# Holding a weight transfer until values have landed, with a third score buffer and earlier gathers, in a fused block-sparse attention and MLP kernel

## The chip, the cores and the metric

One core of a Trainium2 chip runs the kernel. Times are device microseconds of one execution. A kernel is compared by the mean of its fast runs over the mean of the fast runs of the kernel before in the same rounds on the same chip, with a 95% interval. A ratio is therefore not quite the ratio of the medians that stand beside it.

Engines in the profile, by what they do in this kernel: PE multiplies matrices (PEld loads its weights), DVE does elementwise work, ACT exponentials and Gelu, POOL gathers, and SP and POOL issue DMA transfers. SPq and POOLq are the two DMA queues of those two issuers. The argument below takes it that each engine works through its own instructions in program order; where no run below tests this, it is the author's assumption.

## The reference

```python
def _attn_ref(q, k, v, sampled_blocks):          # (4, 8, 768, 64) each; blocks of 32, 24 of them
    scores = np.matmul(q, k.transpose(0, 1, 3, 2)) / np.sqrt(D)
    # kept: neighbouring blocks, first and last block row and column, 3 sampled blocks per block row
    scores = np.where(mask, scores, -1e9)
    attn = softmax(scores)                         # written out in the original
    return np.matmul(attn, v)

def _moe_ref(x, w_in, w_out):                      # x: (3072, 512); w_in: 512 x 2048; w_out: 2048 x 512
    h = x @ w_in
    return gelu_exact(h) @ w_out
```

## The kernel before

A batch of 768 rows is worked in two halves of 384. Each half has attention, then a hidden layer (w_in, Gelu), then an output layer (w_out) whose matmuls are woven between the attention steps of the next half. The first half of batch 0 computes **dense** scores with a mask folded in ("dense half"). Every other half gathers key and value blocks with POOL (tiles kg and v_gat). Values are first cast into `v_flat`, then three rotated copies of them are made by DMA, and the value gathers read those.

The parts that the argument touches:

```python
def load_v(b, eng, after=None):                   # one buffer for the values of a batch
    t = stv_pool.tile([P, NT, H, D], F32, tag="st_v", name="st_v")
    if after is not None:
        after.memset(t[:, :, 0:1, 0:1], 0.0)
    for n in range(NT):                           # rows of 64 f32 = 256 bytes
        eng.dma_start(out=t[:, n], in_=v[b, :, n * P:n * P + P].rearrange("h p d -> p h d"))
    return t
# ...
new_x(0, 0, st)
first_pair(0)                                     # transpose q and k of head pair 0
for c in range(2):
    load_w_in(c)                                  # POOL queue, at about 12 us
gather_iotas()
for hp in range(NPAIR):                           # dense half; first_pt has two buffers (hp % 2)
    for t in range(NT):
        first_scores(hp, t)                       # PE scores, ACT exp
        if t == 1 and hp > 0:
            first_weighted(hp - 1)                # PE: needs the cast values
        elif t == 3 and hp + 1 < NPAIR:
            first_pair(hp + 1)
            if hp == 0:
                for n in range(NT):
                    own_v(0, first_v, n, n + 1, dve)     # casts of batch 0's values
            elif hp == 1: ...                     # index arithmetic on DVE
            elif hp == 2: ...                     # rotation on SP, value indices on DVE
# ...
for c in range(2):
    load_w_out(c)
# ... first second half of attention, main list:
#     S0 D0 S1 E0 W0 D1 S2 E1 W1 D2 S3 E2 W2 D3 E3 W3
#     S scores, D dense scores, E dense weighting (tile od), W gathered weighting (tile og)
after[0] = own_steps(b + 1)                       # right behind S0: two casts of the next batch's
                                                  # values, then their rotation
```

Two buffers serve the results of E and W. E1 can therefore start only when DVE has normalised E0.

The softmax here doesn't subtract the row's maximum and nothing guards it: scores larger than these inputs give would overflow.

Of the kernel before, what the change touches and what calls it, by code (L numbers as in the profile page):

```python
# [11 lines left out]
BF16 = mybir.dt.bfloat16  # L12
# [3 lines left out]
AF = mybir.ActivationFunctionType  # L16
# [3 lines left out]
P = 128  # L20
# [3 lines left out]
NT = S // P  # L24
# [55 lines left out]
def kernel(  # L80
# [34 lines left out]
    def load_qk(b, which, n):  # L115

        t = st_pool.tile([P, NPAIR, NT * D], BF16, tag="st", name="st")
        src = {"q": q, "k": k}[which]
        pool.dma_start(
            out=t, in_=src[b, 4 * n:4 * n + 4].rearrange("h (p j) d -> p h (j d)", j=NT))  # L120
        return t
# [31 lines left out]
    def iota(out, pattern, base, mult):  # L153
        pool.iota(out, pattern=pattern, base=base, channel_multiplier=mult,
                  allow_small_or_imprecise_dtypes=True)
# [5 lines left out]
    def load_w_in(c):  # L161
        f = slice(1024 * c, 1024 * c + 1024)
        pool.dma_start(out=w_in_sb[:, :, f], in_=w_in_v[:, :, f])

    def load_w_out(c):
        pool.dma_start(out=w_out_sb[:, 8 * c:8 * c + 8, :], in_=w_out_v[:, 8 * c:8 * c + 8, :])
# [9 lines left out]
    pool.affine_select(out=ident, in_=ident, compare_op=ALU.not_equal, fill=1.0, base=0,  # L176
                       pattern=[[-1, P]], channel_multiplier=1)
    iota(blocks, [[1, NB]], 0, 0)
    for w, x in (("k", k), ("q", q)):
        pool.dma_start(out=st["st", w, 0][:, 2:4, :],  # L180
                       in_=x[0, 2:4].rearrange("h (p j) d -> p h (j d)", j=NT))
    for w in "kq":
        st["st", w, 1] = load_qk(0, w, 1)



    key_i = small("key_i", [1], I32)
# [50 lines left out]
    mask_x = small("mask_x", [NT, P], BF16, const)  # L238
    n_even = -(-(NULL + 1) * H * GW // DW)

    def gather_iotas():
        iota(mask_ka, [[4, 4], [1, NR]], 0, 0)
        iota(rowm, [[4, 4]], 3, 0)
        iota(cols, [[4, 3]], 3, 0)
        iota(qbt, [[1, NQ], [0, NR]], 1, 0)
        pool.memset(base_v, float(NULL))
        iota(base_v[96:128, 3::4], [[1, 5]], 0, 0)
        iota(base_v[96:128, 2:19:4], [[1, 5]], 7, 0)

    def gather_constants():  # L250

# [116 lines left out]
    def own_v(b, st_v, lo, hi, eng):  # L368
        n = slice(lo, hi)
        cast(eng, v_own[b % 2][:, n, :, 0:D], st_v[:, n])  # L370

    def rotate_v(b, r, eng):

        for lo, hi, src in ((0, P - 32 * r, 32 * r), (P - 32 * r, P, 0)):
            eng.dma_start(out=v_all[lo:hi, NT * r:NT * r + NT],
                         in_=v_own[b % 2][src:src + hi - lo])
# [117 lines left out]
    def dense_weighted(b, hp, st):  # L494

        od = og_pool.tile([P, 1, 2, VW], F32, tag="og", name="od")
        for t in range(NT):
# [3 lines left out]
        normalise(st["xd"][:, hp:hp + 1].rearrange("p m (h d) -> p m h d", h=2), od, 1)  # L501


    first_pt = [first.tile([P, NT, 2, HALF], BF16, name="first_pt"),
                v_gat[0].rearrange("p n h e -> p (n h e)")[:, 0:NT * 2 * HALF]
                .rearrange("p (t h c) -> p t h c", t=NT, h=2)]

    def first_scores(hp, t):
        s1 = sc_pool.tile([P, 2, 512], F32, tag="sc", name="s1")
        c = slice(t * P, t * P + P)  # L510
        for l, r_, first_ in ((onehot.rearrange("p n c -> p (n c)"),
                               barred.rearrange("p n c -> p (n c)"), True),
                              (st["k", hp], st["q", hp], False)):
            for h in range(2):
                r = slice(64 * h, 64 * h + 64)
                pe.matmul(s1[:, h, 0:HALF], lhsT=l[r, c], rhs=r_[r, 0:HALF],
                          start=first_, stop=not first_)
        act.activation(first_pt[hp % 2][:, t], s1[:, :, 0:HALF], AF.Exp, scale=scale)

    def first_weighted(hp):  # L520
        og = og_pool.tile([P, MH, 2, VW], F32, tag="og", name="og")
        for m in range(MH):
            for h in range(2):
                for t in range(NT):
                    pe.matmul(og[:, m, h, :], lhsT=first_pt[hp % 2][:, t, h, m * P:m * P + P],
                              rhs=v_own[0][:, t, 2 * hp + h, 0:VW],
                              start=(m == h == t == 0), stop=True, skip_group_check=True)
        normalise(st["x", 0][:, :, hp * P:hp * P + P].rearrange("p m (h d) -> p m h d", h=2),
                  og, MH)

    def new_x(b, hb, st):
        st["x", hb] = x_pool.tile([P, MH, D_MODEL], BF16, tag="x", name="x")
        st["xT", hb] = x_pool.tile([P, KIN, HALF], BF16, tag="xT", name="xT")
        if hb == (b == 0):
            st["xd"] = x_pool.tile([P, NPAIR, P], BF16, tag="xd", name="xd")
# [90 lines left out]
    def first_pair(hp):  # L626
        i = 2 * (hp % 2)
        for w in "kq":
            pair = st["st", w, hp // 2][:, i:i + 2, :]
            if hp == 0:  # L630
                act.copy(pair, first_st[w])
            transpose_qk(0, hp, w, pair, dve, st)
        for w in "kq":
            globals_qk(0, hp, w, pool, st)

    new_x(0, 0, st)
    first_pair(0)
    for c in range(2):
        load_w_in(c)
    gather_iotas()  # L640
    for hp in range(NPAIR):
        for t in range(NT):
            first_scores(hp, t)
            if t == 1 and hp > 0:
                first_weighted(hp - 1)
            elif t == 3 and hp + 1 < NPAIR:
                first_pair(hp + 1)
                if hp == 0:
                    for n in range(NT):
                        own_v(0, first_v, n, n + 1, dve)  # L650
                elif hp == 1:
                    gather_constants()
                    key_indices()
                    value_columns()
                elif hp == 2:
                    for r in range(1, 4):
                        dve.memset(v_all[:, NT * r:NT * r + 1, 0:1, 0:1], 0.0)
                        rotate_v(0, r, sp)
                    value_indices(0, dve)
                    value_indices(1, dve)  # L660
    first_weighted(NPAIR - 1)
    for m in range(MH):
        transpose_x(0, 0, m, st)
    clear_mask()
    for i in range(2):
        clear_globals(i, dve)
    for c in range(2):
        load_w_out(c)
    for i in range(2):
        mark_valid(i)  # L670
    first_ctx.close()
    g_pool = ctx.enter_context(tc.tile_pool(name="g_pool", bufs=1))
    os_pool = ctx.enter_context(tc.tile_pool(name="os_pool", bufs=3))

    sts[1]["st", "v"] = load_v(1, sp, dve)

    def load_batch(b):
        st = sts[b]
        for n in range(2):
            for w in "kq":  # L680
                st["st", w, n] = load_qk(b, w, n)

    def transpose_step(b, hp):
        i = 2 * (hp % 2)
# [11 lines left out]
    def global_steps(b):  # L696
        return [lambda: [global_v(b, s, dve) for s in range(4)]]
# [4 lines left out]
    for half in range(2 * B):  # L702
        b, hb = divmod(half, 2)
        nb_, nhb = divmod(half + 1, 2)
        more = b + 1 < B

        aux = []
        if half == 0:
            for t in kgl[1]:
                dve.memset(t, 0.0)  # L710
            aux = global_steps(0) + k_steps(0, 1, (0,)) + v_steps(0, 1)
            aux += k_steps(0, 1, range(1, NPAIR))
        elif hb == 0 and more:
            for hp in (0, 1):
                aux += t_steps(b + 1, (hp,)) + k_steps(b + 1, 0, (hp,))
        elif hb == 1 and more:
            if b == 0:
                aux = v_steps(1, 0)
            aux += global_steps(b + 1)
            for hp in range(2 * (b > 0), NPAIR):  # L720
                aux += t_steps(b + 1, (hp,)) + k_steps(b + 1, 0, (hp,))
            if b + 2 < B:
                sts[b + 2]["st", "v"] = load_v(b + 2, sp)
        for n, step in enumerate(spread(hidden_steps(b, hb, sts[b]), aux)):
            step()
        if half == 0:
            load_batch(1)

        fill = output_steps(b, hb, sts[b])
        if half + 1 == 2 * B:  # L730
            weave([], fill)
            break
        main = attention_steps(nb_, nhb, sts[nb_])
        after = {}
        if nhb == 1 and more:
            after[0] = own_steps(b + 1)
            if b > 0:
                after[3] = k_steps(b + 1, 1, (0,))
                after[4] = k_steps(b + 1, 1, (1,))
                after[len(main) - 4] = v_steps(b + 1, 0)  # L740
        elif nhb == 0:
            if nb_ + 1 < B:
                load_batch(nb_ + 1)
            after[0] = v_steps(nb_, 1) + k_steps(nb_, 1, range(2 * (b > 0), NPAIR))
        steps = []
        for n, (step, m) in enumerate(main):
            steps.append((step, m))
            steps += [(f, 0) for f in after.get(n, [])]
        weave(steps, fill)
# [30 lines left out]
```

## Time and profile before

| | before |
|---|---|
| median of 4 runs | 336.98 us (336.42 to 337.69) |
| span of the profiled run | 335.9 us |
| PE busy | 274.0 us, 82% |
| hidden layer 0 starts | 59.16 us |
| E1 starts | 89.17 us |

Stretches of the kernel before, cut at the start of E1. The columns are the stretch, its length, busy time and instructions of each engine, the mean granted PE clock, the DMA engines' mean busy share and GB/s.

```profile
core 0: us, PE busy (x) PEld busy (x) DVE busy (x) ACT busy (x) POOL busy (x), PEclk, DMA share, GB/s
0.00:89.17 89.17, 48.42 (x572) 29.48 (x573) 38.78 (x155) 35.02 (x45) 23.64 (x47) 0.85 0.78 152
89.17:335.90 246.73, 225.63 (x2991) 135.57 (x2988) 101.14 (x209) 120.95 (x161) 78.92 (x103) 1.00 0.38 82
```

PE works 48 of the first 89 us, but 226 of the last 247. About two thirds of PE's idle time (40.8 of 61.9 us) lie ahead of E1.

PE's waits of the kernel before, from 10 to 130 us (what waited, for whom, us in total, times, longest):

```profile
PE og L54 <- DVE v_flat L54: 12.4, 4, 10.0
PE s L54 <- POOL kg L54: 6.8, 1, 6.8
PE s L54 <- DVE v_flat L54: 4.9, 1, 4.9
```

The timeline places these waits (start, duration, engine, instruction, count, idle before it and what ended it). SPq and POOLq lines are transfers being issued.

```profile
2.22 17.09 SPq L54 DMA_DIRECT2D st_v<-in_v_dram  x6
12.38 1.49 POOL L54 DMA_DIRECT2D w_in_sb<-in_moe_w_in_dram  x2
29.41 0.43 DVE L54 CAST v_flat<-st_v 128x512 bf16<-128x512 f32 x1 [9.80 <-DMA st_v<-in_v_dram]
59.16 2.76 PE L54 MATMUL hp<-xT,w_in_sb 128*128 128x384 bf16 x16 [0.52 <-DVE xT L54]
69.70 1.66 POOL L54 INDIRECT_COPY v_gat<-v_flat,idx_v 128x1024 f32 x1 [9.03 <-issue]
80.37 1.10 DVE L54 CAST v_flat<-st_v 128x1536 bf16<-128x1536 f32 x1 [1.60 <-DMA st_v<-in_v_dram]
82.58 0.47 PE L54 MATMUL s<-tq,kg 64*128 64x32 bf16 x22 [6.83 <-POOL kg L54]
89.17 0.51 PE L54 MATMUL od<-v_flat,pd 128*128 128x130 bf16 x6
```

Batch 0's values, issued from 2.22 us, are only 1.6 MB, yet the fourth of their six casts waits until 29.41 and the last starts at 31.37. w_in was issued in between, at 12.38. Later kg makes PE wait until 82.58, because POOL did the value gathers (from 69.70) first. The last line is E1, which had to wait for nothing by itself.

### The profile page before, as it was taken

What the parts mean: (1) busy time and instruction counts of PE and PEld (TensorE: products, weight loads), DVE (VectorE), ACT (ScalarE), POOL (GpSimd) and SP (SyncE); (2) the same over time, 40 slices, a digit from 0 to 9 for tenths busy, and PEclk for the clock granted to TensorE, in tenths of its full rate; (3) what the DMA queues carried; (4) which work ended last, traced back from release to release, by engine and by line L of the source; (5) the groups of instructions that cost most, each with busy time, mean ns of one, the idle gap of its engine ahead of it and who ended that gap; (6) DMA issues with size and microseconds to landing.
All of it is one profiled execution on the core that took longest, in us unless ns stands there. A gap on an engine that the chain in (4) does not pass through costs nothing. (4 is left out here: it accounts for less than half of the span.)

```text
span 335.9 us, 8110 instructions
## 1 busy us (share of the span) xinstructions
PE 274.0 (82%) x3560; PEld 165.1 (49%) x3560; DVE 139.9 (42%) x364; ACT 156.0 (46%) x206; POOL 102.6 (31%) x149
## 2 busy tenths in 40 slices
PE   1712937881989979898999798999997999999995
PEld 0302514441655656464656464555564655555542
DVE  5221795502455727532553177326442453044001
ACT  2430633580542376246625663356346652663420
POOL 4410121134623446444415455232035341000000
PEclk9985878998799999999999999999999999999999
DMA  7996009996999608600769095004910000000001
GB/s 141 208 207 126 3 29 195 232 179 130 246 188 193 106 2 134 119 33 0 176 196 204 3 156 97 31 2 97 257 38 0 35 33 31 2 31 35 31 33 62
DMA packets 42131, 33.79 MB, mean 101 GB/s; under 512 B 26096, under 2 KB 36464, under 8 KB 42096
## 3 DMA queue, kind: packets, MB, share of 16 engines
q1 hardware_dynamic: 31024, 23.18, 28.1%
q0 software_dynamic: 11072, 10.09, 19.4%
q8 instruction: 28, 0.46, 0.6%
q14 instruction: 7, 0.06, 0.1%
HBM read 27.34 MB, written 6.29 MB: 100 GB/s over the span
## 5 line engine op out<-in xcount | busy, mean ns | idle before, releaser
L54 PE MATMUL op<-w_out_sb,g 128*128 128x512 bf16 x384 | 94.8, 383 | 0.0
L54 ACT ACTIVATE g<-hp 128x768 bf16<-128x768 f32 x64 | 51.7, 810 | 84.4 <-PE hp L54 84.4
L54 PE MATMUL hp<-xT,w_in_sb 128*128 128x384 bf16 x512 | 86.8, 327 | 1.6 <-ACT g L54 1.0
L54 PEld LDWEIGHTS <-w_in_sb 128*128 128x128 bf16 x512 | 49.1, 98 | 35.4 <-issue 2.3
L54 ACT ACTIVATE pt<-s 128x1024 bf16<-128x1024 f32 (+2 forms) x84 | 51.6, 687 | 28.0 <-PE s L54 14.4
L54 DVE TENSOR_TENSOR pt<-pt,mask_x 128x768 bf16<-128x768 bf16 x28 | 21.3, 762 | 85.8 <-ACT pt L54 85.7
L54 POOL INDIRECT_COPY kg<-tk,idx_k 128x704 f32 x28 | 34.9, 1248 | 62.8 <-issue 58.6
L54 POOL INDIRECT_COPY v_gat<-v_flat,idx_v 128x1024 f32 (+1 forms) x21 | 33.5, 1594 | 61.6 <-issue 35.3
L54 PEld LDWEIGHTS <-g 128*128 128x128 bf16 x384 | 33.9, 98 | 31.7 <-issue 0.5
L54 DVE COPY tk<-ps 128x768 bf16<-128x768 bf16 x16 | 15.3, 956 | 32.0 <-PE ps L54 32.0
L54 PEld LDWEIGHTS <-tk 64*128 64x128 bf16 (+1 forms) x312 | 15.1, 98 | 26.9 <-issue 19.1
L54 DVE COPY os<-op 128x512 f32<-128x512 f32 x24 | 16.5, 689 | 25.6 <-PE op L54 25.5
L54 ACT ACT_TABLE_LOAD x16 | 20.5, 1283 | 10.9 <-PE hp L54 5.3
L54 PE MATMUL s<-tq,tk 64*128 64x128 bf16 (+1 forms) x216 | 19.6, 260 | 6.2 <-DVE v_flat L54 4.9
L54 PE MATMUL ps<-ident,st 128*64 128x128 bf16 x384 | 15.7, 237 | 9.2 <-ACT st L54 9.2
L54 PE MATMUL s<-tq,kg 64*128 64x32 bf16 x616 | 12.2, 174 | 12.6 <-POOL kg L54 6.8
L54 PEld LDWEIGHTS <-pt 128*32 128x32 bf16 (+1 forms) x868 | 19.9, 97 | 2.9 <-issue 0.6
L54 POOL COPY kgl<-tk 64x64 bf16<-64x64 bf16 x32 | 8.1, 254 | 40.7 <-DVE tk L54 40.0
L54 PEld LDWEIGHTS <-st 128*64 128x64 bf16 x384 | 12.7, 120 | 14.8 <-ACT st L54 9.4
L54 ACT ACTIVATE v_gat<-s 128x768 bf16<-128x768 f32 x12 | 9.0, 809 | 23.1 <-PE s L54 23.1
L54 DVE TENSOR_TENSOR x<-og,rc 128x384 bf16<-128x384 f32 x32 | 17.8, 558 | 1.1
L54 PEld LDWEIGHTS <-kg 64*128 64x128 bf16 x616 | 11.3, 93 | 14.1 <-issue 7.1
(109 smaller groups left out, 241.9 us busy)
## 6 DMA issues: line engine op xcount, KB each, us to landing
st_v<-in_v_dram SPq DMA_DIRECT2D x24, 256.0 KB, 5.9
out_dram<-os SPq DMA_DIRECT2D x24, 256.0 KB, 2.5
v_flat<-v_flat SPq DMA_DIRECT2D x8, 594.0 KB, 7.0
v_flat<-v_flat SPq DMA_DIRECT2D x8, 396.0 KB, 5.5
st<-in_k_dram POOLq DMA_DIRECT2D x7, 384.0 KB, 8.7
st<-in_q_dram POOLq DMA_DIRECT2D x7, 384.0 KB, 10.3
w_in_sb<-in_moe_w_in_dram POOLq DMA_DIRECT2D x2, 1024.0 KB, 13.4
w_out_sb<-in_moe_w_out_dram POOLq DMA_DIRECT2D x2, 1024.0 KB, 22.0
```

Source lines behind the costliest of these rows:

```text
L54: return self._tc.keep_in_program_order(f(*args, **kwargs))
```

## The change

Its intent: let batch 0's values land before w_in starts, by giving w_in's target a small DVE write behind the casts, so that the transfer must wait for it. Keep PE and ACT busy meanwhile by running the scores up to three head pairs ahead of the weighting, in a third buffer (memory of the second gather tile, not yet in use). Bring forward the key gathers, w_out and batch 1's q and k. The diff also moves POOL's index patterns ahead of batch 0's q and k loads, which start about 1 us later for it (2.58 for 1.50 us); this is left out below. The core of the diff:

```diff
-    first_pt = [first.tile(...), v_gat[0]...]
+    first_pt = [first.tile(...)] + [... for t in v_gat]            # cut: three buffers, hp % 3
 ...
+    def after_values():
+        for n in range(NT):
+            own_v(0, first_v, n, n + 1, dve)
+        for c in range(2):
+            dve.memset(w_in_sb[:, 0:1, 1024 * c:1024 * c + 1], 0.0)
+            load_w_in(c)
+    def rotate_first():
+        for r in range(1, 4):
+            dve.memset(v_all[:, NT * r:NT * r + 1, 0:1, 0:1], 0.0)
+            rotate_v(0, r, sp)
     new_x(0, 0, st)
     first_pair(0)
-    for c in range(2):
-        load_w_in(c)
-    gather_iotas()
+    extra = {(0, 3): lambda: first_pair(1),
+             (1, 1): lambda: first_pair(2),
+             (1, 3): lambda: first_pair(3),
+             (2, 1): after_values,
+             (2, 3): lambda: [first_weighted(0), gather_constants(), key_indices()],
+             (3, 1): lambda: [first_weighted(1), load_w_out(0), load_w_out(1)]
+             + [f() for f in k_steps(0, 1, range(NPAIR))],
+             (3, 3): lambda: [first_weighted(2), rotate_first(), value_columns()]}
 ...
     for i in range(2):
         mark_valid(i)
+    load_batch(1)                                  # batch 1's q and k
 ...
-            aux = global_steps(0) + k_steps(0, 1, (0,)) + v_steps(0, 1)
-            aux += k_steps(0, 1, range(1, NPAIR))
+            aux = v_steps(0, 1) + global_steps(0)
 ...
-        if half == 0:
-            load_batch(1)                          # was behind hidden layer 0
```

More of the change, by code (lines that the diff above doesn't have):

```diff
@@ L178 @@
     iota(blocks, [[1, NB]], 0, 0)
-    for w, x in (("k", k), ("q", q)):
-        pool.dma_start(out=st["st", w, 0][:, 2:4, :],
-                       in_=x[0, 2:4].rearrange("h (p j) d -> p h (j d)", j=NT))
-    for w in "kq":
-        st["st", w, 1] = load_qk(0, w, 1)
     key_i = small("key_i", [1], I32)
@@ L239 @@
     n_even = -(-(NULL + 1) * H * GW // DW)
-    def gather_iotas():
-        iota(mask_ka, [[4, 4], [1, NR]], 0, 0)
-        iota(rowm, [[4, 4]], 3, 0)
-        iota(cols, [[4, 3]], 3, 0)
-        iota(qbt, [[1, NQ], [0, NR]], 1, 0)
-        pool.memset(base_v, float(NULL))
-        iota(base_v[96:128, 3::4], [[1, 5]], 0, 0)
-        iota(base_v[96:128, 2:19:4], [[1, 5]], 7, 0)
+    iota(mask_ka, [[4, 4], [1, NR]], 0, 0)
+    iota(rowm, [[4, 4]], 3, 0)
+    iota(cols, [[4, 3]], 3, 0)
+    iota(qbt, [[1, NQ], [0, NR]], 1, 0)
+    pool.memset(base_v, float(NULL))
+    iota(base_v[96:128, 3::4], [[1, 5]], 0, 0)
+    iota(base_v[96:128, 2:19:4], [[1, 5]], 7, 0)
+    for w, x in (("k", k), ("q", q)):
+        pool.dma_start(out=st["st", w, 0][:, 2:4, :],
+                       in_=x[0, 2:4].rearrange("h (p j) d -> p h (j d)", j=NT))
+    for w in "kq":
+        st["st", w, 1] = load_qk(0, w, 1)
     def gather_constants():
@@ L501, in dense_weighted @@
         normalise(st["xd"][:, hp:hp + 1].rearrange("p m (h d) -> p m h d", h=2), od, 1)
-    first_pt = [first.tile([P, NT, 2, HALF], BF16, name="first_pt"),
-                v_gat[0].rearrange("p n h e -> p (n h e)")[:, 0:NT * 2 * HALF]
-                .rearrange("p (t h c) -> p t h c", t=NT, h=2)]
+    first_pt = [first.tile([P, NT, 2, HALF], BF16, name="first_pt")]
+    for t in v_gat:
+        first_pt.append(t.rearrange("p n h e -> p (n h e)")[:, 0:NT * 2 * HALF]
+                        .rearrange("p (t h c) -> p t h c", t=NT, h=2))
     def first_scores(hp, t):
@@ L517, in first_scores @@
                           start=first_, stop=not first_)
-        act.activation(first_pt[hp % 2][:, t], s1[:, :, 0:HALF], AF.Exp, scale=scale)
+        act.activation(first_pt[hp % 3][:, t], s1[:, :, 0:HALF], AF.Exp, scale=scale)
     def first_weighted(hp):
@@ L524, in first_weighted @@
                 for t in range(NT):
-                    pe.matmul(og[:, m, h, :], lhsT=first_pt[hp % 2][:, t, h, m * P:m * P + P],
+                    pe.matmul(og[:, m, h, :], lhsT=first_pt[hp % 3][:, t, h, m * P:m * P + P],
                               rhs=v_own[0][:, t, 2 * hp + h, 0:VW],
@@ L634, in first_pair @@
             globals_qk(0, hp, w, pool, st)
-    new_x(0, 0, st)
-    first_pair(0)
-    for c in range(2):
-        load_w_in(c)
-    gather_iotas()
-    for hp in range(NPAIR):
-        for t in range(NT):
-            first_scores(hp, t)
-            if t == 1 and hp > 0:
-                first_weighted(hp - 1)
-            elif t == 3 and hp + 1 < NPAIR:
-                first_pair(hp + 1)
-                if hp == 0:
-                    for n in range(NT):
-                        own_v(0, first_v, n, n + 1, dve)
-                elif hp == 1:
-                    gather_constants()
-                    key_indices()
-                    value_columns()
-                elif hp == 2:
-                    for r in range(1, 4):
-                        dve.memset(v_all[:, NT * r:NT * r + 1, 0:1, 0:1], 0.0)
-                        rotate_v(0, r, sp)
-                    value_indices(0, dve)
-                    value_indices(1, dve)
-    first_weighted(NPAIR - 1)
-    for m in range(MH):
-        transpose_x(0, 0, m, st)
-    clear_mask()
-    for i in range(2):
-        clear_globals(i, dve)
-    for c in range(2):
-        load_w_out(c)
-    for i in range(2):
-        mark_valid(i)
-    first_ctx.close()
-    g_pool = ctx.enter_context(tc.tile_pool(name="g_pool", bufs=1))
-    os_pool = ctx.enter_context(tc.tile_pool(name="os_pool", bufs=3))
-    sts[1]["st", "v"] = load_v(1, sp, dve)
     def load_batch(b):
@@ L681, in load_batch @@
                 st["st", w, n] = load_qk(b, w, n)
+    def after_values():
[8 more added lines that the diff above has]
+            rotate_v(0, r, sp)
+    new_x(0, 0, st)
+    first_pair(0)
+    extra = {(0, 3): lambda: first_pair(1),
[6 more added lines that the diff above has]
+             (3, 3): lambda: [first_weighted(2), rotate_first(), value_columns()]}
+    for hp in range(NPAIR):
+        for t in range(NT):
+            first_scores(hp, t)
+            extra.get((hp, t), lambda: None)()
+    first_weighted(NPAIR - 1)
+    for m in range(MH):
+        transpose_x(0, 0, m, st)
+    value_indices(0, dve)
+    value_indices(1, dve)
+    clear_mask()
+    for i in range(2):
+        clear_globals(i, dve)
+    for i in range(2):
+        mark_valid(i)
+    load_batch(1)
+    first_ctx.close()
+    g_pool = ctx.enter_context(tc.tile_pool(name="g_pool", bufs=1))
+    os_pool = ctx.enter_context(tc.tile_pool(name="os_pool", bufs=3))
+    sts[1]["st", "v"] = load_v(1, sp, dve)
     def transpose_step(b, hp):
```

## The prediction

> **What bounds the kernel now.** The span is 335.9 us; PE is busy 82% (page, part 1). The stretch table puts nearly all idle PE time before 83 us: about 44 of the first 83 us busy, later stretches near full. The timeline and the waits name the holes:
> - 19.9 to 31.9: PE waits for the casts of the first batch's values, DVE for their transfers (11.9 us in four waits). Six value transfers issued from 2.2 us land up to 18.9 us after issue; the last three only when w_in has landed (issued 12.4, landing after 10.9 and 16.0 us).
> - 43.5 to 48.4: PE waits 4.9 us behind DVE's index arithmetic.
> - 75.7 to 82.6: PE waits 6.8 us for kg, which stands on POOL behind three value gathers that started at 69.7, after the rotation (issued 48.4 to 54.8) had landed beside w_out.
>
> Hidden layer 0 starts at 59.2, the first gathered weighting of its second half at 83.9, the second dense weighting (E1) at 89.2. From there PE is full, so the change is worth what it takes off E1.
>
> **Why values starve.** [...] beside w_in (2048 B) the values (256 B) move 24 against 182 GB/s; beside st (768 B) 50 against 140; rotation (6336 B) against w_out (1024 B) 200 against 45.
>
> **What the change does.** w_in waits for the casts; all pairs are transposed early; scores run three pairs ahead of the weighting; key gathers go ahead of the value gathers; w_out follows w_in at once; batch 1's q and k load at about 50 us instead of 89. Added work is two tiny memsets (0.06 us each). PE, ACT and DVE work stays.
>
> Estimates from these durations: values land at about 20 us, casts end at 25 (6 x 0.43), w_in is issued at 25 to 26. 24 exponentials of 0.755 us and the PE work between them end the dense half at about 35; value columns (4.5 us, now ahead of the last normalise) put hidden layer 0 at 42 to 44 (59.2 before). Rotation is issued at 34 to 36 and lands at 48 to 52; value gathers end at 58 to 62 (77.8 before). The 6.8 us wait for kg goes.
>
> **What catches the gain.** The transfers become one busy stretch from 26 us: w_in 2.1 MB, rotation 2.4, w_out 2.1, batch 1's q/k 1.6, its values 1.6. At the observed 165 to 250 GB/s this is about 49 us, so batch 1's values, starved behind w_out and q/k, land at about 76 (80.4 before). Their casts stand in DVE's order ahead of the second mask and the normalise that frees E1's buffer. So E1 starts at about 79, 10 us earlier rather than 16; PE idles some 8 to 10 us before it and restarts at a reduced clock (as at 80 to 90 us before, mean 0.66), costing about 2 us. Net 8 to 9 us.
>
> **Predicted: 328.5 us, range 321 to 334; faster by over 2% 0.68, within 2% 0.28, slower 0.04.**
>
> **What would show it.** No wait for st_v over 3 us before 30 us; w_in issued near 25; hidden layer 0 near 43; kg waits gone; a new DVE wait for batch 1's st_v landing near 76, and PE waiting for DVE in the second half's attention until about 79; unchanged stretches after it.
>
> **What would make it wrong.** If batch 1's values land before about 70 the gain is 13 to 16 us; if q/k and w_out starve them past 82, it is under 5. A late w_in (second half after 49 us)[...] would also cost.

The rates under "Why values starve" are worked out from the packet records of the kernel before. The sum: 10 us at E1 less about 2 for the clock, net 8 to 9, hence 328.5.

## The result, and the profile after

| | before | after | predicted |
|---|---|---|---|
| median of 4 runs | 336.98 us | 327.64 us (325.92 to 328.57) | 328.5 (321 to 334) |
| ratio of fast runs | | 0.9716 (0.9666 to 0.9765) | |
| span of the profiled run | 335.9 | 324.2 | |
| hidden layer 0 starts | 59.16 | 39.69 | 42 to 44 |
| last value gather of batch 0 ends | 77.75 | 60.63 | 58 to 62 |
| E1 starts | 89.17 | 75.65 | 79 |

The profiled run after was the fastest of the four, and the profiled run before (337.77 us, not one of the four in the table) was slower than all of those. So the gain in span (11.7 us) is larger than the gain of the medians (9.3 us).

The two stretches after, cut at E1 again:

```profile
0.00:75.65 75.65, 46.59 (x573) 27.14 (x574) 39.99 (x155) 36.70 (x48) 25.20 (x51) 0.87 0.98 178
75.65:324.20 248.55, 227.31 (x2988) 136.52 (x2987) 104.30 (x212) 119.11 (x158) 74.92 (x98) 0.99 0.35 82
```

E1 comes 13.5 us earlier, and what follows E1 takes 1.8 us longer (248.55 against 246.73). The DMA share ahead of E1 rose from 0.78 to 0.98. A share can exceed 1 (it is 1.13 from 38 to 52 us), so this doesn't mean that there was no pause: from 20 to 24 us, while w_in is held, it is 0.02.

PE's waits after, from 10 to 130 us:

```profile
PE od L54 <- DVE xd L54: 8.3, 1, 8.3
PE psx L54 <- DVE x L54: 3.6, 1, 3.6
PE hp L54 <- ACT g L54: 3.3, 1, 3.3
```

The waits for values, for kg and for the index arithmetic are gone. Three others took their place. The largest is E1 (tile od) waiting for DVE's normalise of E0 (tile xd). The timeline after shows where that comes from:

```profile
21.10 2.17 DVE L54 CAST v_flat<-st_v 128x512 bf16<-128x512 f32 x6
23.60 1.48 POOL L54 DMA_DIRECT2D w_in_sb<-in_moe_w_in_dram  x2 [1.61 <-DVE w_in_sb L54]
39.69 5.28 PE L54 MATMUL hp<-xT,w_in_sb 128*128 128x384 bf16 x16 [0.52 <-DVE xT L54]
50.39 0.06 DVE L54 MEMSET st_v<- 128x6 f32 x1
50.48 19.70 SPq L54 DMA_DIRECT2D st_v<-in_v_dram  x6
52.58 1.65 POOL L54 INDIRECT_COPY v_gat<-v_flat,idx_v 128x1024 f32 x1 [5.36 <-DVE vgl L54]
70.67 0.96 DVE L54 CAST v_flat<-st_v 128x1536 bf16<-128x1536 f32 x1 [8.99 <-DMA st_v<-in_v_dram]
73.76 0.96 DVE L54 CAST v_flat<-st_v 128x1536 bf16<-128x1536 f32 x1 [2.13 <-DMA st_v<-in_v_dram]
74.64 0.55 DVE L54 TENSOR_TENSOR pt<-pt,mask_x 128x768 bf16<-128x768 bf16 x1
75.30 0.29 DVE L54 TENSOR_TENSOR xd<-od,rc 128x128 bf16<-128x128 f32 x1
75.65 0.81 PE L54 MATMUL od<-v_flat,pd 128*128 128x130 bf16 x6 [8.29 <-DVE xd L54]
```

Batch 0's six casts now follow each other without a wait, and hidden layer 0 starts 19.5 us earlier. But the next batch's values are late: DVE stands idle 8.99 us and 2.13 us for them. Its next instructions, a mask and the normalise (xd), wait behind the casts, and PE waits for xd.

Why the values are late is seen in the packet records of the two traces, from which these rates are worked out (GB/s by target, each transfer known by its row size):

```
stretch                     values (256 B)   the other stream
before, 18 to 27 us              24          w_in   (2048 B)  182
before,  9 to 14 us              50          q and k (768 B)  142
after,  58 to 67 us              48          q and k (768 B)  142
after,  37 to 47 us               -          rotation (6336 B) 207 beside w_out (1024 B) 36
after,  68 to 73 us             182          nearly alone
```

The trace's records are single rows, and in the first three stretches the two queues moved about equal numbers of them: the profile counts 816, 951 and 1721 records for POOL's queue and 838, 982 and 1721 for SP's. The ratios of the rates there follow the row sizes: 24:182 is 0.13 (256:2048 is 0.125), and 50:142 is 0.35 (256:768 is 0.33). Rotation beside w_out, 5.7 for 6.2, fits too. The counts are not equal in every stretch: from 68 to 72 us before, batch 1's values beside w_out moved 64 against 138 GB/s, with 1003 records to 546. What sets the shares is not shown. In these stretches the stream of short rows gets the lower rate beside the stream of long rows, whichever was issued first (values at 2.22 us and w_in at 12.38 before; q and k from 44.18 and values from 50.48 after).

Starvation is not all of the lateness. SP issues batch 1's values only at 50.48 us, once DVE has come to the small write in front of them (50.39 us; the line with `after` in load_v), which stands behind DVE's index and mask work. From the first issue to the last landing (73.64 us) they then take 23.2 us. The runs below give a scale: 16.7 us in qk1_held, where w_out alone is beside them, and 9.0 us in free_held, where neither w_out nor q and k are. Moving that write forward was not tried.

### The profile page after: what moved, and what is told of

Its sections match the earlier page's. It is cut to its first block, busy times and chain, and to the rows that moved or that the text cites. A ratio compares the mean times of both kernels' runs of the same rounds, so it can differ in the third digit from the quotient of the medians.

```text
span 324.2 us, 8106 instructions
## 1 busy us (share of the span) xinstructions
PE 273.9 (84%) x3560; PEld 163.7 (50%) x3560; DVE 144.3 (45%) x366; ACT 155.8 (48%) x206; POOL 100.1 (31%) x149
## 5 line engine op out<-in xcount | busy, mean ns | idle before, releaser
L54 PE MATMUL hp<-xT,w_in_sb 128*128 128x384 bf16 x512 | 91.0, 337 | 3.8 <-ACT g L54 3.3
L54 PEld LDWEIGHTS <-w_in_sb 128*128 128x128 bf16 x512 | 50.4, 100 | 40.3 <-issue 8.8
L54 POOL INDIRECT_COPY kg<-tk,idx_k 128x704 f32 x28 | 33.7, 1204 | 68.6 <-issue 56.3
L54 ACT ACT_TABLE_LOAD x16 | 20.5, 1283 | 18.8 <-DVE idx_v L54 13.2
L54 DVE COPY os<-op 128x512 f32<-128x512 f32 x24 | 16.5, 687 | 23.3 <-PE op L54 23.2
L54 ACT ACTIVATE pd<-sd 128x768 bf16<-128x768 f32 x16 | 13.0, 816 | 17.9 <-PE sd L54 17.9
L54 PE MATMUL s<-tq,tk 64*128 64x128 bf16 (+1 forms) x216 | 18.4, 250 | 1.3 <-ACT pt L54 0.7
L54 PE MATMUL psx<-ident,x 128*128 128x128 bf16 x96 | 9.8, 227 | 10.4 <-DVE x L54 3.6
L54 PE MATMUL od<-v_flat,pd 128*128 128x130 bf16 x96 | 8.5, 227 | 9.3 <-DVE xd L54 8.8
```

Of the source, the lines that this page charges most:

```text
L54: return self._tc.keep_in_program_order(f(*args, **kwargs))
```

## The experiments

All gave correct outputs. All were timed in three rounds against the kernel before (337 to 338 us in each set). E1 is the start of the second dense weighting in the profiled run. One profile per kernel says little about an E1 to within 1 us or so: kg_first changes nothing ahead of E1 against rot_early, and its E1 is 1.3 us later.

| kernel | median us | ratio to before (95%) | E1 us |
|---|---|---|---|
| the change | 327.64 | 0.9716 (0.9666 to 0.9765) | 75.65 |
| hold_alone | 327.68 | 0.9706 (0.9665 to 0.9748) | 79.46 |
| w_in_free | 326.10 | 0.9659 (0.9627 to 0.9690) | 77.42 |
| g_free | 326.90 | 0.9701 (0.9665 to 0.9737) | 75.36 |
| qk1_late | 322.84 | 0.9527 (0.9483 to 0.9570) | profile slow |
| own_late | 326.41 | 0.9675 (0.9633 to 0.9717) | 67.52 |
| qk1_held | 321.02 | 0.9505 (0.9466 to 0.9544) | 68.96 |
| free_held | 327.58 | 0.9704 (0.9664 to 0.9743) | 75.29 |
| qk1_held_g_free | 320.56 | 0.9483 (0.9439 to 0.9527) | 67.93 |
| rot_early | 317.68 | 0.9419 (0.9377 to 0.9462) | 63.93 |
| hold_kg | 326.70 | 0.9661 (0.9619 to 0.9704) | 76.15 |
| kg_first | 319.75 | 0.9442 (0.9376 to 0.9509) | 65.25 |
| kg_first_mid | 319.82 | 0.9482 (0.9426 to 0.9539) | 64.26 |

**The theory.** The change removes about 24 us of PE stalls ahead of E1 (12.4 + 6.8 + 4.9), but the gain is capped by when batch 1's values land. They starve beside w_out (39 against 157 GB/s from 54.5 to 56.5 us) and batch 1's q and k (48 against 142 from 58 to 67), and DVE's order passes their lateness on to E1. **Rivals:** holding w_in back is itself what gains; hidden layer 0 (with its two new waits) is on the path; E1 waits for w_out or for the gathers.

### hold_alone: the smallest part of the change

```diff
 # on the kernel before
-    for c in range(2):
-        load_w_in(c)
 ...
                     for n in range(NT):
                         own_v(0, first_v, n, n + 1, dve)
+                    for c in range(2):
+                        dve.memset(w_in_sb[:, 0:1, 1024 * c:1024 * c + 1], 0.0)
+                        load_w_in(c)
```

> The kernel before with one edit: w_in waits, through the two small writes, for the casts of the first batch's values. No third score buffer, no other reordering. My theory (the changed kernel's gain is capped by when batch 1's values land, so most of its reordering buys nothing): casts end near 22 us instead of 31.8, hidden layer 0 starts near 50 (59.2 before), E1 (second dense weighting) near 80 (89.2 before), total 326 to 330 us, that is the whole gain of the change or nearly. Rival (the third buffer and the early key gathers are needed for most of the gain): 332 to 336 us.

Measured: 327.68 us, the same as the whole change. The last cast of batch 0's values starts at 21.08 us (31.37 before), hidden layer 0 at 49.19, E1 at 79.46:

```profile
79.46 0.51 PE L54 MATMUL od<-v_flat,pd 128*128 128x130 bf16 x6
```

Holding w_in for batch 0's values gives 9.6 us by itself. The rest of the change adds nothing on top of it as it stands, although it brings hidden layer 0 another 9.5 us forward. Of these, 3.8 us reach E1 in the profiles, and what follows E1 takes 1.4 us longer (248.6 for 247.2). The medians show nothing of the remainder; the change's profile is of its fastest run.

### w_in_free: the change without the hold on w_in

```diff
 # on the changed kernel
         for c in range(2):
-            dve.memset(w_in_sb[:, 0:1, 1024 * c:1024 * c + 1], 0.0)
-            load_w_in(c)
+            dve.memset(w_out_sb[:, 8 * c:8 * c + 1, 0:1], 0.0)
 ...
     first_pair(0)
+    for c in range(2):
+        load_w_in(c)
```

> The changed kernel with w_in issued at the start again (near 10 us); w_out is held until the casts instead. My theory: values starve until about 30 us and PE gets a hole of about 7 us before the first weighting; hidden layer 0 starts near 47 (39.7 in the changed kernel); but the transfers as a whole end earlier, batch 1's values land near 67, and E1 starts near 74 (75.7 in the changed kernel), so the total is within 2 us of the changed kernel, 325 to 329 us. Rival (holding w_in back is what gains): slower than the changed kernel by 5 us or more, 332 us or above.

Measured: 326.10 us, with hidden layer 0 at 49.12. The hole is back (PE waits 5.4 us for batch 0's values), yet the time is no worse, because E1 no longer waits for batch 1's values: both their casts run together at 71.83. With three buffers and no hold on w_in, or with the hold and two buffers, the result is the same 326 to 328 us. Two steps of my theory failed, though the total fell in the range: batch 1's values landed at 72.3, not 67 (they were issued only from 59.5), and E1 came at 77.4, not 74. w_out is held here instead of w_in, so this is not quite the change without any hold.

### g_free: take a wait away that should not count

In the changed kernel the first Gelu waits for the last value index, since the Gelu's tile takes over the memory of the index tiles.

```diff
 # on the changed kernel; the same for base_v, lane, step, own
-    idx_vf = msk.tile([P, 2, 6], F32, name="idx_vf")
+    idx_vf = const.tile([P, 2, 6], F32, name="idx_vf")
```

> The changed kernel with the index tiles of the value gathers kept outside the memory that the hidden activations g take over, so that the first Gelu need not wait for the last index. In the changed kernel that wait is 13.2 us of ACT and 3.3 us of PE at 45 to 48 us. My theory: hidden layer 0 ends 3 to 5 us earlier but stands in the shadow of batch 1's values; E1 still starts near 75.6 and the total stays within 1.5 us of the changed kernel's. Rival (hidden layer 0 with its reduced clock and this wait is on the path): faster by 3 to 5 us, 322 to 324 us.

Measured: 326.90 us (change 327.64), nothing that the intervals separate. In its timeline E0 starts 1.9 us earlier (61.28 for 63.22), but E1 still stands at 75.36, after a wait of 8.07 us for xd. Time won in hidden layer 0 is lost again at E1: that rival falls.

### qk1_late: take q and k of batch 1 out of the values' way

```diff
 # on the changed kernel
         mark_valid(i)
-    load_batch(1)
 ...
             step()
+        if half == 0:
+            load_batch(1)
```

> The changed kernel with batch 1's q and k loads put back where the kernel before has them, behind the value gathers (near 61 us on POOL instead of 44). My theory: batch 1's values no longer queue behind q and k, land near 64 (about 73 in the changed kernel), PE's 8.3 us wait before E1 nearly goes, E1 starts near 67.5, total 316 to 320 us. Rival (E1 is held by w_out or by the value gathers, or values starve behind w_out alone): total within 2 us of the changed kernel's 327.

Measured: fast runs of 320.57, 320.95, 322.84 and 324.57 us, and one of 328.23 that counts as slow (its clock, 0.968, is no lower than that of two of the fast ones, so it may be the kernel's own; with it the mean is 323.4). The mean is 2% below the change (0.9527 for 0.9716), so the values' neighbours on the DMA do matter. It fell short of the 316 to 320 that I expected, and the runs scatter. The only profile taken is that of the slow run, so it is not compared. In it the last value transfer landed only at 73 us, behind q and k issued from 61.17. Whether the other runs' scatter has this cause is not shown, but it suggested the next kernel, where no such race can occur.

### qk1_held: hold q and k of batch 1 until the values are cast

```diff
 # on the changed kernel
-    load_batch(1)
 ...
+        if after is not None:                      # in load_qk
+            after.memset(t[:, 0:1, 0:1], 0.0)
 ...
             after[0] = own_steps(b + 1)
+            if b == 0:
+                after[0].append(lambda: load_batch(1, dve))
```

> The changed kernel with batch 1's q and k loads held, by the same small write, until the casts of batch 1's values: nothing on that queue can then overtake the last value transfer, as it did in the profiled run of qk1_late (last value transfer issued near 61 us, q and k from 61.2, landing 12.3 us after issue). My theory (batch 1's values landing, through DVE's order, is the cap): values land near 62.5, second cast ends near 64, E1 starts at 67 to 68, total 315.5 to 318.5 us and little spread between runs. Rival (qk1_late's gain came from something else, for instance less traffic beside the rotation): about the same as qk1_late, 320 to 324 us.

Measured: 321.02 us, with runs from 320.75 to 321.66: the scatter is gone and 6.6 us of the change's time with it. E1 starts at 68.96 and its wait is 2.2 us. The second cast, E1, and PE's waits from 10 to 130 us:

```profile
67.04 0.96 DVE L54 CAST v_flat<-st_v 128x1536 bf16<-128x1536 f32 x1 [3.32 <-DMA st_v<-in_v_dram]
68.96 0.51 PE L54 MATMUL od<-v_flat,pd 128*128 128x130 bf16 x6 [2.22 <-DVE xd L54]
PE s L54 <- POOL kg L54: 4.0, 3, 2.9
PE psx L54 <- DVE x L54: 3.6, 1, 3.6
PE hp L54 <- ACT g L54: 3.3, 1, 3.3
PE od L54 <- DVE xd L54: 2.2, 1, 2.2
```

This shows the cap. I had expected 315.5 to 318.5. Two things are missing from that. The second cast started at 67.04, not 63: the last two of the six value transfers were issued only at 60.26 and 61.19, and the last landed at 66.92 (w_out's last packet ended at 59.8 by the packet records, 58.6 in the changed kernel). What holds SP's issuing back is open. And 4.0 us of waits for kg appeared, of which own_late tells more.

### own_late: is it DVE's order?

```diff
 # on the changed kernel
-            after[0] = own_steps(b + 1)
+            after[0 if b else 12] = own_steps(b + 1)
```

> The changed kernel with only the casts and the rotation of batch 1's values moved later in the program (behind the third gathered weighting of that half); transfers are untouched. If E1 waits because DVE's order puts the casts ahead of the normalise that frees its buffer, E1 starts near 67.3 with values landing at 73 as before, so PE's 8.3 us wait goes. But the same landing gates a second deadline: the rotation of batch 1, then three value gathers and the first key gather on POOL (ending near 104 us in the changed kernel), which the next half's scores would now want near 96. I expect most of the wait to come back there (about 7 us on kg), total 323 to 327 us. Rival (only DVE's order matters): 316 to 319 us.

Measured: 326.41 us. No load was changed (the rotation moves with the casts, from 74.78 to 77.47 us), and the last value lands at 74.82, but E1 starts at 67.52 without any wait: what held it was the place of the casts in DVE's order. The gain came back as a wait of 7.5 us at the start of batch 1:

```profile
67.52 0.51 PE L54 MATMUL od<-v_flat,pd 128*128 128x130 bf16 x6
104.87 0.48 PE L54 MATMUL s<-tq,kg 64*128 64x32 bf16 x22 [7.45 <-POOL kg L54]
```

The same landing has a second deadline. Values, casts, rotation, three value gathers and only then kg stand in POOL's order, and batch 1's first scores want that kg. Moving the consumer alone does not help here; the transfer has to come earlier.

### free_held: are the two holds independent?

This joins the edits of w_in_free and qk1_held.

> w_in_free and qk1_held together: w_in from the start, batch 1's q and k held until the casts of batch 1's values. In w_in_free E1 started at 77.4 without waiting for batch 1's values, because the dense half itself ended late (hidden layer 0 at 49.1). If the two caps are separate, taking the second away gains nothing while the first stands: 324.5 to 327.5 us (w_in_free 326.1), against 321.0 of qk1_held. Then holding w_in back is worth about 5 us, but only where q and k do not overtake the values. Rival (holding w_in back is worth nothing in any case): 320 to 322.5 us.

Measured: 327.58 us, 0.1 us outside the range and far from the rival's. With qk1_held, w_in_free and the change it makes a square:

| medians, us | w_in from the start, w_out held | w_in held |
|---|---|---|
| batch 1's q and k issued at about 44 to 54 us | 326.10 | 327.64 |
| q and k held until batch 1's values are cast | 327.58 | 321.02 |

Neither hold alone gives anything. Both together are 5.1 us below neither, and 6.6 us below either alone: with one of the two caps standing, removing the other is invisible.

### qk1_held_g_free and rot_early: what is on the path once the cap is gone

qk1_held_g_free joins qk1_held and g_free.

> qk1_held and g_free together. g_free alone moved nothing, in the shadow of the cap. With the cap gone hidden layer 0 should be on the path: E1 near 65 to 66, total 314 to 317 us, 1 to 2.5 us below qk1_held. If g_free still moves nothing, the values' landing near 62.5 (or the value gathers that end near 60.6) still binds.

Measured: 320.56 us against 321.02; the intervals overlap, so g_free still shows nothing for certain. E1 came 1.0 us earlier (67.93), but PE then waited 3.4 us for w_out, a wait that qk1_held did not have.

```diff
 # rot_early, on qk1_held_g_free
         for n in range(NT):
             own_v(0, first_v, n, n + 1, dve)
+        rotate_first()                             # in after_values, ahead of w_in
 ...
-             (1, 3): lambda: first_pair(3),
-             (2, 1): after_values,
+             (1, 3): lambda: [after_values(), first_pair(3)],
-             (3, 3): lambda: [first_weighted(2), rotate_first(), value_columns()]}
+             (3, 3): lambda: first_weighted(2)}
 ...
         transpose_x(0, 0, m, st)
+    value_columns()
```

> qk1_held_g_free with the first batch's casts moved ahead of the last pair's transposes, the rotation issued right behind them ahead of the weights, and the value columns behind the last normalise of the dense half. This should remove PE's 3.6 us hole at 34 to 38 us and let hidden layer 0 begin near 36 to 37, but the transfers bind then (first batch's rotation, w_in, w_out and batch 1's values are 8.2 MB, about 38 us at 215 GB/s, from about 22 us on): values still land near 60 to 62 and w_out near 55. I expect E1 near 64 to 65 and 313 to 316 us, at most 2 us below qk1_held_g_free.

The 215 GB/s are the author's estimate; the trace after moved 217 GB/s from 40 to 60 us, and rot_early itself 192 from 20 to 40 and 210 from 40 to 60.

Measured: 317.68 us (317.41 to 318.83), the fastest of all: 0.9419 of the kernel before. The 3.6 us hole went, but hidden layer 0 began at 40.79, not 36 to 37: PE's two largest waits are now for w_in and for kg:

```profile
PE hp L54 <- DMA w_in_sb<-in_moe_w_in_dram: 4.4, 1, 4.4
PE s L54 <- POOL kg L54: 3.6, 2, 3.0
```

The gain over qk1_held_g_free was larger than expected (2.9 us for at most 2), the level 2 us higher. Both follow from that kernel being slower than I thought.

### hold_kg: could the kernel before have had this without the third buffer?

```diff
 # on hold_alone
-            aux = global_steps(0) + k_steps(0, 1, (0,)) + v_steps(0, 1)
-            aux += k_steps(0, 1, range(1, NPAIR))
+            aux = global_steps(0) + k_steps(0, 1, range(NPAIR)) + v_steps(0, 1)
```

> hold_alone (the kernel before, w_in held until the casts, two score buffers, q and k of batch 1 late) with one more edit: the other three key gathers of the first second half stand on POOL ahead of the value gathers. It asks what the change could have had without its third buffer and early transposes. In hold_alone PE waits 6.7 us for kg and E1 starts at 79.5. My theory: POOL's gathers as a whole are then the chain (four key gathers from 49.5 to about 61, three value gathers to about 71), so the first gathered weighting moves from 74 to about 71 and E1 to about 76.5: total 323 to 326 us, clearly above the 317.7 us of rot_early. If it reaches 320 us or less, the third buffer was not needed.

Measured: 326.70 us, 0.7 above the range, with E1 at 76.15 as worked out. Simply moving key gathers forward there gives about 1 us, which lies within the intervals. Only kernels with the third buffer and the early transposes reached 318 to 321 us. That the buffer itself is needed is not shown: no run took it alone out of rot_early, and w_out is also issued earlier there.

### kg_first and kg_first_mid: two misses

```diff
 # kg_first, on rot_early
-            if b == 0:
-                aux = v_steps(1, 0)
 ...
                 aux += t_steps(b + 1, (hp,)) + k_steps(b + 1, 0, (hp,))
+                if b == 0 and hp == 1:
+                    aux += v_steps(1, 0)
 # kg_first_mid, on kg_first: rotate_first() moved from after_values to behind first_weighted(0)
```

> rot_early with the value gathers of batch 1 moved on POOL behind its first two key gathers. In rot_early PE waits 3.6 us for kg when batch 1's first half begins, the second deadline that own_late showed (7.6 us there). If that is what is left of it, the wait goes and the total is 313.5 to 315.5 us (rot_early 317.7). If the value gathers become late for the weighting instead, it stays at 317 or rises.

> kg_first with the first batch's rotation issued about 3 us later, behind the first weighting, so that w_in has the transfers to itself for longer. In rot_early PE waits 4.4 us for w_in at 36 to 41 us, while the value gathers wait for their indices (2.9 us), not for the rotation. Sharing about 3 to 1 beside the rotation, w_in should land about 2 us earlier: total 1 to 2 us below kg_first. If w_out or the values of batch 1 bind by then, the same as kg_first.

The 3 to 1 can be seen in the trace after from 36.5 to 37.5 us, when rotation moved 241 GB/s and w_in 82.

Measured: 319.75 and 319.82 us, both slower than rot_early by medians, with the intervals overlapping. In kg_first's profile the kg waits fell from 3.6 only to 2.3 us (they moved to the later head pairs), a wait of 1.7 us for v_gat came, and E1 waited 2.1 us for xd (this is not the edit's doing, which lies behind E1). POOL's gathers as a whole seem to be late there, so that their order only moves the wait. One is busy 1.2 to 1.7 us, but they start about 3.0 to 3.7 us apart (kg at 32.53, 35.89, 39.14 and 42.48 us, v_gat at 52.58, 56.24 and 59.20 in the changed kernel). The profile's spans on POOL are rough, so part of the spacing may be the copy itself. The spacing, not the busy time, is what POOL's order has to be counted with here. In kg_first_mid the wait for w_in went as intended (hidden layer 0 at 36.86) and a 5.3 us wait for the first Gelu took its place. Neither is a better version.

## Why the prediction was right

- **What bound the kernel before:** right. The three holes named are gone, and hold_alone shows the first to be worth 9.6 us.
- **Starvation beside longer rows:** right as far as rates can show; how queues share is not shown. The rates after repeat those before (48 against 142 beside q and k), and qk1_held, which takes that neighbour away, brings E1 6.7 us forward.
- **The cap:** right, and tested from both sides. The busy stretch was predicted as 49 us from 26; by the packet records it runs from 25.1 us to the last value packet at 73.0, 48 us. Values were predicted at about 76; the second cast could start at 73.76. E1 was predicted at 79 and came at 75.65. This term was mis-sized by 3 us in the change's favour, from the start (casts ended at 23.3, not 25) and from the stretch. The prediction names starvation alone as the reason; that SP issues the values only at 50.48 us, behind DVE's small write, is not in it.
- **The reduced clock:** predicted at about 2 us; the stretch behind E1 is 1.8 us longer than before. In the trace after, the granted clock halves in the wait for E1 (the columns are those of the stretches above; the third from the end is the granted clock):

```profile
65.60:69.10 3.50, 1.75 (x37) 0.94 (x35) 0.00 (x0) 2.52 (x4) 0.00 (x0) 1.00 1.27 217
69.20:75.60 6.40, 0.00 (x0) 0.00 (x0) 2.77 (x6) 0.03 (x1) 0.00 (x0) 0.50 0.51 98
75.70:79.20 3.50, 3.50 (x41) 2.18 (x41) 2.65 (x7) 0.00 (x0) 0.00 (x0) 0.50 0.98 221
79.40:80.00 0.60, 0.60 (x9) 0.41 (x7) 0.00 (x0) 0.12 (x1) 0.00 (x0) 1.00 0.95 249
```

  PE's last matmul ahead of the wait ends at 67.35 us, and from 69.1, 1.7 us later, the granted clock is 0.50; in the 3.5 us just ahead of that PE was busy for 1.75. The clock stays at 0.50 until 79.3, the first 3.7 us of the work behind E1; in the kernel before it was back at 1.00 by 87.5, ahead of E1. Hidden layer 0 saw the same: PE was busy without a break from 39.69 to 44.97 us, and the granted clock was 0.50 throughout and until 45.2. What sets these times is not shown. Its first 16 matmuls took 5.28 us at 0.50 and 2.76 us at 1.00 in the kernel before, 1.9 times as long. As an estimate from this, half of 3.7 us, or 1.8, was lost. That the whole 1.8 us is due to it was not tested.
- **What was not foreseen:** the first Gelu's wait for the index tiles (13.2 us of ACT, 3.3 of PE). The 3.6 us hole behind the value columns was in the prediction's sum (4.5 us ahead of the last normalise), not among its waits. Both cost nothing here, since they lie in the shadow of the cap. g_free shows it for the first; for the second it is only argued.
- **The sum:** the profiled run gained 11.7 us where 8 to 9 were predicted, the medians 9.3. The median thus lies closer to the prediction than its own terms do: in the run where E1 can be seen, the sum was 3 us too cautious. That the medians agree so well may be partly luck: E1 in the runs without a profile is not known.

What the change is worth was hence set by one landing, not by the 19.5 us that hidden layer 0 gained. Of the latter, 13.5 reached E1 in the profiled run.

## What to carry to other kernels

When a tuned kernel's transfers are all moved forward, ask which transfer is then last in the queue and which engine's program order passes its lateness on. Here a change that removed 24 us of stalls gained no more than three lines of it alone, until one more load was held back. In these traces a transfer of short rows starved beside one of long rows on another queue (256 B at 24 GB/s beside 2048 B at 182, from 18 to 27 us before). Here it paid to hold the long-rowed one, by a write to its target, until the short-rowed one had landed (9.6 us in hold_alone). Test caps in pairs, since removing one of two shows nothing.
